# A real transform of 576 points along D, split 9 x 64 on VectorE and TensorE instead of 6 x 96 on TensorE and VectorE

## The chip, the core and the metric

The kernel runs on one core of one Trainium2 chip. The metric is the device time of one execution in microseconds (us). An execution also leaves a profile: start and duration of every instruction on TensorE (PE for its products, PEld for the loads of its stationary operand), VectorE (DVE), ScalarE (ACT), GpSimd (POOL) and of every DMA issued from the queues of SP, ACT and POOL.

## The reference, cut to what matters

The program computes the output and all gradients of a gated mix of two branches over a 2048 x 576 activation `x`: a spectral branch (a real 2-D Fourier transform over both axes, a product with complex weights, and the transform back) and a gated feed-forward branch with a hidden width of 4608.

```python
def _A_ref(x, w_r, w_i):
    X = rfft2(x.astype(float32), axes=(-2, -1))
    X = X * (w_r + 1j * w_i)
    return irfft2(X, s=(S, D), axes=(-2, -1)).astype(bfloat16)

def _B_ref(x, w_gate, w_up, w_down):
    return (gelu(x @ w_gate) * (x @ w_up)) @ w_down

g = sigmoid((x * gate_w).sum(-1, keepdims=True))
out = g * _A_ref(x, ...) + (1 - g) * _B_ref(x, ...)
```

The backward pass needs the forward transform twice: of `x`, and of the incoming gradient scaled by the gate `g`. In both cases 16 row tiles of 128 rows are transformed, 32 in all, and the change is in that transform's part along D (576 points, 289 kept frequencies, real and imaginary).

## The kernel before

The program has two phases. The first takes 18 groups `g` of 256 hidden columns, four steps `m` each, 72 steps `pr` in all; a step handles 512 rows. Each step issues on TensorE, in a fixed order: the products for `z` (L466, L471), the products for the hidden activations `xy` (L475, L482), and then a list of jobs that build weight gradients of the group before in `wps` (L594, L612, L626). The second phase (from about 915 us) turns the hidden gradients back into activations (L1228).

The spectral branch rides along in the first phase as small units, called one by one from a list (`fft_next`). A forward row tile has two units. `u1` (L651 to L662) multiplies the row tile with a cosine and sine table over the rows: six products (L656), one for each residue class of the column number modulo 6, into a PSUM tile `pf`, which ScalarE copies to `Z` (L659 for `x`, L661 for the gradient). `u2` (L664 to L698) multiplies `Z` with the table over the columns, six products again (L670), ScalarE copies the sums to `ve` in fp32 (L676), and VectorE combines the six parts in 17 instructions (L678 to L697) into `Vt`, from where a DMA on SP's queue stores it (L698). The six classes are picked out of the natural rows beforehand by a ScalarE copy that reads every sixth element (`sort`, L727 for `x`, L729 for the gradient, where the gate is multiplied in).

What orders the work: all instructions of an engine run in program order, and the program order is written out by hand. Per step there are three units in this stage: one in the middle of the second half of `xy` (`between`, L1084), the others spread over the list of jobs by their weights (L1112 to L1116). How many units a step gets is said by `want` from the list `FIRST` (L950: none in steps 0 to 6, one by step 7, three by step 8) and a line from there. The sorting of a unit's rows is issued a step ahead by `sort_ahead` (L971), behind the copies of `z` (L494) or behind the last unit of the step.

One detail carries the rest: `z` and all `pf` tiles share one PSUM buffer (pool `pz`, one buffer of two banks; L458 and L645). TensorE cannot begin a `z` or a unit until the last reader of the one before has finished. The `wps` and `xy` tiles have two buffers each.

The tables are built at the start: `iotas` (L61), `build_F` (L120, VectorE work at the start, two ScalarE sines in step 6).

Of the kernel before, what the change touches and what calls it, by code (L numbers as in the profile page):

```python
# [9 lines left out]
ACT = mybir.ActivationFunctionType  # L10
ALU = mybir.AluOpType
BF16 = mybir.dt.bfloat16
F32 = mybir.dt.float32
I32 = mybir.dt.int32
MAGIC = 12582912.0
EPS_SCALE = 1.0 - 3e-7
# [3 lines left out]
S, D, DF = 2048, 576, 289  # L20
P, T = 128, 16
# [16 lines left out]
LO, HI = slice(0, 64), slice(64, 128)  # L38
LQ = 49
SIN60 = math.sqrt(0.75)  # L40


def eo(c):
# [18 lines left out]
def iotas(nc, res, unit):  # L62
    tb = Tables()
    G, V = nc.gpsimd, nc.vector
    kw = dict(allow_small_or_imprecise_dtypes=True)
    tb.halfpi = res.tile([P, 1], F32, name="halfpi")
    V.memset(tb.halfpi[:], math.pi / 2)
    tb.pi = res.tile([P, 1], F32, name="pi")
    V.memset(tb.pi[:], math.pi * EPS_SCALE)
    tb.warm = res.tile([P, 1], F32, name="warm")  # L70
    nc.scalar.activation(tb.warm[:], tb.halfpi[:], ACT.Sigmoid)
    tb.lrow = unit([LQ], F32, name="lrow")
    G.iota(tb.lrow[:], pattern=[[1, LQ]], base=0, channel_multiplier=0, **kw)
    tb.dcol = res.tile([P, 6], F32, name="dcol")
    for k, (r, step, n) in enumerate(((1, 1, 2), (0, 0, 1), (5, -1, 3))):
        k0 = (0, 2, 3)[k]
        G.iota(tb.dcol[:, k0:k0 + n], pattern=[[step, n]], base=r, channel_multiplier=6, **kw)
    tb.late = []
    tb.Rt = []
    return tb  # L80
# [39 lines left out]
def build_F(nc, tb, unit):  # L120

    V = nc.vector
    step = 2.0 * math.pi / D
    X = unit([6, LQ], F32, name="XF")
    y = unit([6, LQ], F32, name="yF")
    V.tensor_tensor(X[:], tb.dcol[:].unsqueeze(2).to_broadcast([P, 6, LQ]), tb.lrow[:].unsqueeze(1).to_broadcast([P, 6, LQ]), op=ALU.mult)
    V.tensor_scalar(y[:], X[:], 1.0 / D, MAGIC, op0=ALU.mult, op1=ALU.add)
    V.tensor_scalar(y[:], y[:], -MAGIC, -float(D), op0=ALU.add, op1=ALU.mult)
    V.tensor_tensor(X[:], X[:], y[:], op=ALU.add)
    V.scalar_tensor_tensor(y[:], X[:], -1.0, X[:], op0=ALU.mult, op1=ALU.max)  # L130
    tb.F = unit([6, 2, LQ], name="Ft")

    def sines():
        nc.scalar.activation(tb.F[:, :, 0], y[:], ACT.Sin, bias=tb.halfpi[:], scale=-step)
        nc.scalar.activation(tb.F[:, :, 1], X[:], ACT.Sin, scale=-step * EPS_SCALE)
    tb.late.append(sines)


# [153 lines left out]
def kernel(  # L292
# [4 lines left out]
    nc = tc.nc  # L297
    LD = nc.sync
    ST = nc.gpsimd
    V = nc.vector  # L300
    ctx.enter_context(tc.manual_schedule())
    kw = dict(reuse_waits="tile")
    dram = ctx.enter_context(tc.tile_pool(name="dram", bufs=1, space=DRAM))
    res = ctx.enter_context(tc.tile_pool(name="res", bufs=1))
    unit = Unit(ctx.enter_context(tc.tile_pool(name="unit", bufs=NUNIT, side="right")), "unit")
# [25 lines left out]
    xn = wstack.enter_context(tc.tile_pool(name="pxn", bufs=1)).tile([P, T, D], BF16, name="xn")  # L331
# [51 lines left out]
    tb = iotas(nc, res, unit)  # L383
# [17 lines left out]
    g32 = res.tile([P, T], F32, name="g32")  # L401
# [244 lines left out]

    def fwd_units(src, dst, scale):
        zs = {}
        CLS = (1, 2, 0, 5, 4, 3)

        def u1(t):  # L651
            def f():
                zps = pftile()
                row = src.pop(t)
                for k, r in enumerate(CLS):
                    nc.tensor.matmul(zps[0:96, k // 3, k % 3 * P:(k % 3 + 1) * P], lhsT=row[:, r], rhs=tb.Rt[t], start=True, stop=True)  # L656
                zs[t] = unit([2, 3 * P], name="Z")
                if scale is None:
                    nc.scalar.copy(zs[t][0:96], zps[0:96, :, 0:3 * P])  # L659
                else:  # L660
                    nc.scalar.activation(zs[t][0:96], zps[0:96, :, 0:3 * P], ACT.Copy, scale=scale)  # L661
            return f  # L662

        def u2(t):  # L664
            def f():
                Z = zs.pop(t)
                vps = pftile()
                w = 2 * LQ
                for k in range(6):
                    nc.tensor.matmul(vps[:, k // 3, k % 3 * w:(k % 3 + 1) * w], lhsT=Z[0:96, k // 3, k % 3 * P:(k % 3 + 1) * P],  # L670
                                     rhs=tb.F[0:96, k].rearrange("p c l -> p (c l)"), start=True, stop=True)
                Vt = half([2, DF], name="Vt")
                ve = unit([2, 3, 2, LQ], F32, name="ve")
                sd = unit([2, 3, 2, LQ], F32, name="sd")
                M = unit([6, 2, LQ], F32, name="vm")
                nc.scalar.copy(ve[:].rearrange("p b k c l -> p b (k c l)"), vps[:, :, 0:3 * w])  # L676
                lo, hi = ve[:, 0], ve[:, 1]
                V.tensor_tensor(sd[:, 0], lo, hi, op=ALU.add)  # L678
                V.tensor_tensor(sd[:, 1, :, 0], hi[:, :, 0], lo[:, :, 0], op=ALU.subtract)
                V.tensor_tensor(sd[:, 1, :, 1], lo[:, :, 1], hi[:, :, 1], op=ALU.subtract)  # L680
                e, o = sd[:, 0, 2], sd[:, 1, 2]
                for k, op in enumerate((ALU.add, ALU.subtract)):
                    V.tensor_tensor(M[:, k], sd[:, 0, 0], sd[:, 0, 1], op=op)
                    V.tensor_tensor(M[:, 4 + k, 1::-1], sd[:, 1, 0], sd[:, 1, 1], op=op)
                p_, m_ = M[:, 0], M[:, 1]
                for c, op in enumerate((ALU.subtract, ALU.add)):
                    V.scalar_tensor_tensor(M[:, 2, c], m_[:, c], 0.5, o[:, c], op0=ALU.mult, op1=op)
                V.scalar_tensor_tensor(M[:, 3], p_, -0.5, e, op0=ALU.mult, op1=ALU.add)
                up = Vt[:, :, 96:DF - 1].rearrange("p c (j l) -> p j c l", j=2)[:, :, :, 0:LQ]
                dn = Vt[:, :, 1:193].rearrange("p c (j l) -> p j c l", j=2)[:, :, :, 94:47:-1]  # L690
                V.tensor_tensor(Vt[:, :, 0:LQ], e, p_, op=ALU.add)
                V.scalar_tensor_tensor(Vt[:, 0, DF - 1:DF - LQ:-1], o[:, 0, 0:LQ - 1], -1.0, m_[:, 0, 0:LQ - 1], op0=ALU.mult, op1=ALU.subtract)
                V.tensor_tensor(Vt[:, 1, DF - 1:DF - LQ:-1], m_[:, 1, 0:LQ - 1], o[:, 1, 0:LQ - 1], op=ALU.subtract)
                for c in range(2):
                    V.scalar_tensor_tensor(up[:, :, c], M[:, 4:6, c], SIN60, M[:, 2:4, c], op0=ALU.mult, op1=ALU.add)
                for c, s_, op in ((0, -SIN60, ALU.add), (1, SIN60, ALU.subtract)):
                    V.scalar_tensor_tensor(dn[:, :, c], M[:, 4:6, c, 1:LQ - 1], s_, M[:, 2:4, c, 1:LQ - 1], op0=ALU.mult, op1=op)  # L697
                LD.dma_start(dst[:, t], Vt[:])  # L698
            return f
        first = [u1(t) for t in range(T)]  # L700
        for t, u in enumerate(first):
            u.sort = (src, t)
        return first, [u2(t) for t in range(T)]

    xq, gq, graw = {}, {}, {}
# [2 lines left out]
        f.noslot = True  # L708
        return f

    def classes(dst, k):
        q = unit([2, 6, 96], name="xq")
        for j in range(2):
            dst[2 * k + j] = q[:, j]
        return q

    def load_g(k):
        def f():
# [2 lines left out]
        return noslot(f)  # L721

    def sort(dst, t):
        if t % 2 == 0:
            classes(dst, t // 2)
        if dst is xq:
            nc.scalar.copy(xq[t], xn[:, t, :].rearrange("p (q r) -> p r q", r=6))  # L727
        else:
            nc.scalar.activation(gq[t], graw[t // 2][:, t % 2].rearrange("p (q r) -> p r q", r=6), ACT.Copy, scale=g32[:, t:t + 1])  # L729

    def turned():
        tp_ = pftile(BF16)
# [159 lines left out]
    for c in range(6):  # L892
        w = gwr[0:1, eo(c)] if c < 4 else gwr[0:1, 512:D]
        r = slice(0, P) if c < 4 else (LO, HI)[c - 4]
# [52 lines left out]
    mid_at = 4 * T + 8  # L947
    NPR = NT // 2
    LASTP = NG * NPR - 7
    FIRST = (0, 0, 0, 0, 0, 0, 0, 1, 3)  # L950
    done = [0]

    def want(pr):
# [12 lines left out]
        return int(min(n, n_slots) + 1e-9)  # L966

    slots = [u for u in fft if not getattr(u, "noslot", False)]
    sorted_to = [0]

    def sort_ahead(pr):  # L971
        to = want(pr + 1) if pr + 1 < NG * NPR else n_slots
        due = [u.sort for u in slots[sorted_to[0]:to] if hasattr(u, "sort")]
        sorted_to[0] = max(to, sorted_to[0])
        n = int(pr != 7)
        for q in due[:n]:
            sort(*q)
        return due[n:]

    wgT_all = []  # L980

# [18 lines left out]
    for g in range(NG):  # L1000
# [3 lines left out]
        for m in range(NPR):  # L1004
            pr = g * NPR + m
            n = want(pr) - done[0]
# [64 lines left out]
            else:  # L1071
# [8 lines left out]
                k0 = int(n > 0 and pr > 7 and ready())  # L1080
# [23 lines left out]
                at, k, free = 0.0, k0, 0.0  # L1104
# [4 lines left out]
                if pr == 8:  # L1109
                    last = 1.2  # L1110
                    due = [d - last for d in due]
# [88 lines left out]
    with tc.tile_pool(name="p2f", bufs=3, **kw) as p2f, \  # L1200
# [36 lines left out]
        vp, ft, zt = {}, {}, {}  # L1237
# [239 lines left out]
```

## Time and profile before

| | us |
|---|---|
| median of the runs | 1361.12 (1360.99 to 1361.24, 3 runs) |
| the profiled execution: its own time | 1361.22 |
| its span, first to last instruction | 1359.4 |
| PE busy | 1343.9 (99%) |
| DVE busy | 879.5 (65%) |
| ACT busy | 771.0 (57%) |
| stretch with the forward units, 85 to 367 us: PE / DVE / ACT busy of 282.0 | 279.4 / 247.0 / 231.5 |

A row of the groups reads: line, engine, operation, output<-inputs, shape, count, then the busy time of the group, the mean of one, and the idle time of the engine just before. A row of the timeline reads: start, length, engine, line, what, and in square brackets the idle time of the engine before it and who ended it. Products are pipelined, so the records of two of them overlap; the time from start to start is what TensorE spends on one.

### The profile page before, as it was taken

How to read it: one execution, taken by the hardware profiler on the slowest of the kernel's cores; microseconds unless marked ns; L12 is line 12 of the kernel's file. 1: busy time of each engine (PE TensorE's matmuls, PEld its weight loads, DVE VectorE, ACT ScalarE, POOL GpSimd, SP SyncE). 2: the span in 40 equal slices, each digit the busy share in tenths (PEclk: the TensorE clock that was granted, in tenths of full speed). 3: DMA queues.
4: the chain of work that ended last, by engine and by line, in shares of the span. 5: the costliest groups of instructions: out<-in, count | busy, mean ns of one | idle time of the engine just before them, and what ended most of it. 6: DMA issues, size and time to landing. Idle time of an engine off the chain costs nothing.

```text
span 1359.4 us, 26947 instructions
## 1 busy us (share of the span) xinstructions
PE 1343.9 (99%) x10279; PEld 901.0 (66%) x10360; DVE 879.5 (65%) x2351; ACT 771.0 (57%) x1380; POOL 244.1 (18%) x488
## 2 busy tenths in 40 slices
PE   9999999999999999999999999999999999999999
PEld 6556656656655656655655655558888888888887
DVE  6988888888857876876776855526543455354420
ACT  5797888888767776776777666622332232232210
POOL 3011111110313633434433311100000000000000
PEclk9999999999999999999999999999999999999999
DMA  9624435534554644644754657499999787888773
GB/s 222 174 71 133 138 98 150 157 99 133 138 144 115 175 121 117 171 119 121 174 140 115 163 123 181 120 238 237 201 204 216 160 175 160 168 164 173 155 155 74
DMA packets 493606, 207.05 MB, mean 152 GB/s; under 512 B 313346, under 2 KB 485444, under 8 KB 493476
## 3 DMA queue, kind: packets, MB, share of 16 engines
q1 hardware_dynamic: 467330, 170.47, 55.1%
q0 software_dynamic: 15040, 24.38, 6.2%
q10 hardware_dynamic: 11106, 10.48, 3.1%
q8 instruction: 81, 1.33, 0.4%
q14 instruction: 49, 0.40, 0.1%
HBM read 41.18 MB, written 89.11 MB: 96 GB/s over the span
## 4 chain that ended last, share of the span: by engine, by line
PE 98%; DVE 1%; issue 1%; ACT 0%; ACTq 0%; DVEq 0%
PE acc L1228 31%; PE wps L612 18%; PE xy L482 18%; PE wps L594 10%; PE z L466 9%; PE wps L626 2%; PE xy L475 2%; PE z L471 2%; PE pf L656 1%; PE acc L1280 1%; PE pf L670 1%; PE acc L1290 1%; PE pf L856 1%; PE pf L778 1%; PE pf L419 0%
## 5 line engine op out<-in xcount | busy, mean ns | idle before, releaser
L1228 PEld LDWEIGHTS <-pin 128*128 128x128 bf16 x3456 | 334.7, 98 | 82.7
L482 PE MATMUL xy<-wgu,xT 128*128 128x512 bf16 x1082 | 257.8, 380 | 8.6 <-issue 7.4
L612 PE MATMUL wps<-dH,xn 128*128 128x512 bf16 x1141 | 263.8, 379 | 0.6
L612 PEld LDWEIGHTS <-xn 128*128 128x128 bf16 x1152 | 111.2, 98 | 125.5 <-issue 0.6
L482 PEld LDWEIGHTS <-xT 128*128 128x128 bf16 x1152 | 105.5, 98 | 133.2 <-issue 25.2
L594 PE MATMUL wps<-dB,A 128*128 128x288 bf16 x1152 | 149.9, 286 | 0.0
L619 POOL DMA_DIRECT2D out_dram<-dw x134 | 73.1, 549 | 423.5 <-ACT dw L563 411.8
L1228 PE MATMUL acc<-wgT,pin 128*128 128x288 bf16 x1152 | 146.6, 286 | 0.0
L1228 PE MATMUL acc<-wd_all,pin 128*128 128x288 bf16 x1152 | 146.4, 286 | 0.0
L1228 PE MATMUL acc<-wuT,pin 128*128 128x288 bf16 x1152 | 146.1, 286 | 0.0
L1292 ACT ACTIVATE yo<-acc 128x288 bf16<-128x288 f32 x64 | 67.4, 1245 | 132.2 <-PE acc L1290 113.3
L466 PE MATMUL z<-wdT,dOT 128*128 128x256 bf16 x1152 | 138.0, 273 | 0.9 <-ACT dOT L438 0.8
L594 PEld LDWEIGHTS <-A 128*128 128x128 bf16 x1152 | 111.7, 98 | 33.0
L494 ACT ACTIVATE da<-z,omg 128x256 bf16<-128x256 f32 x288 | 111.9, 471 | 28.3 <-PE z L471 28.1
L466 PEld LDWEIGHTS <-dOT 128*128 128x128 bf16 x1152 | 112.3, 98 | 22.6 <-issue 0.5
L1408 DVE TENSOR_TENSOR b16t<-acc,f32t 128x288 bf16<-128x288 f32 x32 | 14.7, 458 | 168.4 <-PE acc L1228 168.3
L503 ACT CAST xb<-xy 128x512 bf16<-128x512 f32 x144 | 85.6, 594 | 38.7 <-PE xy L482 38.0
L1282 ACT CAST Z<-acc 98x384 bf16<-98x384 f32 x64 | 27.5, 481 | 113.1 <-PE acc L1280 113.1
L504 ACT CAST hu<-xy 128x512 bf16<-128x512 f32 x144 | 87.9, 610 | 0.0
L540 DVE TENSOR_TENSOR xb<-xb,sg 128x1024 bf16<-128x1024 bf16 x48 | 33.1, 690 | 80.8 <-ACT sg L532 80.8
L501 ACT ACTIVATE q<-xy 128x512 bf16<-128x512 f32 x144 | 80.4, 606 | 3.3 <-PE xy L482 3.0
L563 ACT CAST dw<-wps 128x512 bf16<-128x512 f32 x72 | 42.2, 588 | 60.1 <-PE wps L612 42.8
(513 smaller groups left out, 1807.6 us busy)
## 6 DMA issues: line engine op xcount, KB each, us to landing
scr<-dH SPq DMA_DIRECT2D x144, 256.0 KB, 3.4
scr<-A SPq DMA_DIRECT2D x72, 256.0 KB, 2.4
out_dram<-dw POOLq DMA_DIRECT2D x134, 64.0 KB, 1.9
wd_all<-in_B_w_down_dram SPq DMA_DIRECT2D x3, 1728.0 KB, 12.6
out_dram<-dwd POOLq DMA_DIRECT2D x34, 144.0 KB, 2.9
scr_p<-Vt SPq DMA_DIRECT2D x32, 144.5 KB, 2.9
Vp<-scr_p ACTq DMA_DIRECT2D x32, 144.5 KB, 4.3
wgu<-in_B_w_gate_dram SPq DMA_DIRECT2D x18, 256.0 KB, 4.3
```

Source lines behind the costliest of these rows:

```text
L466: nc.tensor.matmul(zo(t), lhsT=dOT[:, ci, t, :], rhs=wdT[:, ci, :], start=(t % 4 < 2 and ci == 0), stop=False)
L482: nc.tensor.matmul(xy[k][:, t % 2, :], lhsT=xT[:, ci, t, :], rhs=wgu[:, ci, :], start=False, stop=(ci == 3))
L494: nc.scalar.activation(da[:, t, :], z[:, t % 2, t // 2, :], ACT.Copy, scale=omg32[:, 4 * m + t:4 * m + t + 1])
L501: nc.scalar.activation(q[:, h, :], xy[:, :, 0:FG], ACT.Square)
L503: nc.scalar.copy(xb[:, h, :], xy[:, :, 0:FG])
L504: nc.scalar.copy(hu[:, h, :], xy[:, :, FG:2 * FG])
L563: wcopy[0](out, in_)
L594: nc.tensor.matmul(wps[:, :288], lhsT=tl(0, t)[:, fch * P:(fch + 1) * P], rhs=dB[:, t, h * 288:(h + 1) * 288], start=(t == 0), stop=(t == ...
L612: nc.tensor.matmul(wps[:].rearrange("p a b -> p (a b)"), lhsT=xn[:, t, c * P:(c + 1) * P], rhs=kt[t // 4][1][:, t % 4].rearrange("p k f -> ...
L619: wst[0].dma_start(ov[:, c, fsl], dw[:, k, :])
L1228: nc.tensor.matmul(acc[:, :288], lhsT=src[:, r, :], rhs=w_of(r)[:, h * 288:(h + 1) * 288], start=(first and r == 0), stop=(last and r == F ...
L1292: nc.scalar.activation(yv[:, 3 * b:3 * b + 3], ps[:, 0:288].rearrange("p (r q) -> p r q", r=3), ACT.Copy, scale=(SD2, 1.0)[w])
```

## The change

The split of D becomes 9 x 64. The nine-point part moves to the front: `sort` no longer copies; VectorE computes the nine-point transform of two natural row tiles at a time from `xn` or `graw`, in `nine_a` (sums and cosines, 14 instructions) for the even tile of the pair and `nine_b` (differences and sines, 10 instructions) for the odd one, in fp32, into a tile `xq` of 64 + 4 x 128 columns per row. For the gradient, ScalarE first scales both natural rows of the pair in place. `u1` then has five products with 128 stationary columns, and two ScalarE copies into `Z` (512 and 128 columns). `u2` has four products of 128 columns with the rotations in the table and one of 66. There is no combining on VectorE any more: two ScalarE copies write `Vt` straight from PSUM, in frequency order, so that both step through `Vt` in steps of nine elements. The tables are built to match, `FIRST` becomes nine zeros, and `sort_ahead` counts sorts instead of slots (pairs are completed, and at most one sort is done beyond the need).

```diff
-                for k, r in enumerate(CLS):
-                    nc.tensor.matmul(zps[0:96, k // 3, k % 3 * P:(k % 3 + 1) * P], lhsT=row[:, r], rhs=tb.Rt[t], start=True, stop=True)
-                zs[t] = unit([2, 3 * P], name="Z")
-                if scale is None:
-                    nc.scalar.copy(zs[t][0:96], zps[0:96, :, 0:3 * P])
...
+                for k in (1, 2, 3, 4, 0):
+                    c0 = 128 * k - (64 if k else 0)
+                    nc.tensor.matmul(zps[:, int(k == 0), max(k - 1, 0) * P:max(k, 1) * P], lhsT=row[:, c0:c0 + P], rhs=tb.Rt[t], start=True, stop=True)
+                Z = zs[t] = unit([5 * P], name="Z")
+                for b, c in enumerate((slice(0, 4 * P), slice(4 * P, 5 * P))):
+                    if scale is None:
+                        nc.scalar.copy(Z[:, c], zps[:, b, 0:c.stop - c.start])
...
-                for k in range(6):
-                    nc.tensor.matmul(vps[:, k // 3, k % 3 * w:(k % 3 + 1) * w], lhsT=Z[0:96, k // 3, k % 3 * P:(k % 3 + 1) * P],
-                                     rhs=tb.F[0:96, k].rearrange("p c l -> p (c l)"), start=True, stop=True)
+                o = vps[:, 0].rearrange("p (c o q) -> p c o q", c=2, o=8)
+                for k in range(1, 5):
+                    nc.tensor.matmul(o[:, :, k - 1:9 - k:9 - 2 * k, :], lhsT=Z[:, (k - 1) * P:k * P],
+                                     rhs=tb.F[:, (k - 1) * P:k * P].rearrange("p (c h q) -> p c h q", c=2, h=2), start=True, stop=True)
+                nc.tensor.matmul(vps[:, 1, 0:66], lhsT=Z[:, 4 * P:5 * P], rhs=tb.F[:, 512:578], start=True, stop=True)
                 Vt = half([2, DF], name="Vt")
-                nc.scalar.copy(ve[:].rearrange("p b k c l -> p b (k c l)"), vps[:, :, 0:3 * w])
...
+                nc.scalar.copy(Vt[:, :, 0:DF - 1].rearrange("p c (q o) -> p c o q", o=9)[:, :, 1:9, :], o)
+                nc.scalar.copy(Vt[:, :, 0:DF:9], vps[:, 1, 0:66].rearrange("p (c q) -> p c q", c=2))
                 LD.dma_start(dst[:, t], Vt[:])
...
+    def nine_a(q, x, d):
+        Y = unit([3, 2, 64], F32, name="nY")
+        W = unit([3, 2, 64], F32, name="nW")
+        sm = unit([4, 2, 64], F32, name="nS")
+        s3, e, m, sg = (sm[:, k] for k in range(4))
+        V.tensor_tensor(Y[:], x[:, 1:8:3], x[:, 8:1:-3], op=ALU.add)
+        V.tensor_tensor(s3, x[:, 3], x[:, 6], op=ALU.add)
+        V.tensor_tensor(e, x[:, 0], s3, op=ALU.add)
+        V.scalar_tensor_tensor(m, s3, -0.5, x[:, 0], op0=ALU.mult, op1=ALU.add)
+        V.tensor_tensor(W[:, 0:2], Y[:, 0:2], Y[:, 1:3], op=ALU.subtract)
+        V.tensor_tensor(W[:, 2], Y[:, 2], Y[:, 0], op=ALU.subtract)
+        V.tensor_tensor(sg, Y[:, 0], Y[:, 1], op=ALU.add)
+        V.tensor_tensor(sg, sg, Y[:, 2], op=ALU.add)
+        V.tensor_tensor(q, e, sg, op=ALU.add)
+        V.scalar_tensor_tensor(d[:, 2, :, 0], sg, -0.5, e, op0=ALU.mult, op1=ALU.add)
+        V.scalar_tensor_tensor(Y[:], W[:], C1, m.unsqueeze(1).to_broadcast([P, 3, 2, 64]), op0=ALU.mult, op1=ALU.add)
+        for k, j in ((0, 0), (1, 1), (3, 2)):
+            V.scalar_tensor_tensor(d[:, k, :, 0], W[:, (j + 1) % 3], -C2, Y[:, j], op0=ALU.mult, op1=ALU.add)
...
     def sort(dst, t):
-        if t % 2 == 0:
-            classes(dst, t // 2)
-        if dst is xq:
-            nc.scalar.copy(xq[t], xn[:, t, :].rearrange("p (q r) -> p r q", r=6))
-        else:
-            nc.scalar.activation(gq[t], graw[t // 2][:, t % 2].rearrange("p (q r) -> p r q", r=6), ACT.Copy, scale=g32[:, t:t + 1])
+        k, h = t // 2, t % 2
+        if h == 0:
+            q = pairs[k] = unit([2, D], name="xq")
+            for j in range(2):
+                dst[2 * k + j] = q[:, j]
+                if dst is gq:
+                    nc.scalar.activation(graw[k][:, j], graw[k][:, j], ACT.Copy, scale=g32[:, 2 * k + j:2 * k + j + 1])
+        q = pairs[k]
+        x = xn[:, 2 * k:2 * k + 2, :] if dst is xq else graw[k][:]
+        (nine_a, nine_b)[h](q[:, :, 0:64], x.rearrange("p t (j r) -> p j t r", j=9),
+                            q[:, :, 64:D].rearrange("p t (k v r) -> p k t v r", k=4, v=2))
...
-    FIRST = (0, 0, 0, 0, 0, 0, 0, 1, 3)
+    FIRST = (0,) * 9
...
-        due = [u.sort for u in slots[sorted_to[0]:to] if hasattr(u, "sort")]
+        need = sum(1 for u in slots[:to] if hasattr(u, "sort"))
+        need += need % 2
+        to = max(need, min(sorted_to[0] + 1, need + 1, len(sorts)) if pr > 6 else 0)
+        due = sorts[sorted_to[0]:to]
         sorted_to[0] = max(to, sorted_to[0])
-        n = int(pr != 7)
-        for q in due[:n]:
+        for q in due[:1]:
             sort(*q)
-        return due[n:]
+        return due[1:]
```

In `iotas` and `build_F`, four iotas on POOL become eight with four small memsets on VectorE, the column table has 578 columns instead of 6 x 2 x 49, and ScalarE makes one sine over 578 columns and two scaled copies instead of two sines over 294.

More of the change, by code (lines that the diff above doesn't have):

```diff
@@ L40 @@
 SIN60 = math.sqrt(0.75)
+C1, C2 = (math.cos(2.0 * math.pi * k / 9) for k in (1, 2))
+S1, S4 = (math.sin(2.0 * math.pi * k / 9) / SIN60 for k in (1, 4))
+TURN = 4.0 * MAGIC
 def eo(c):
@@ L71, in iotas @@
     nc.scalar.activation(tb.warm[:], tb.halfpi[:], ACT.Sigmoid)
[L72 to L77, printed above, removed]
+    ft = tb.ft = unit([P], F32, name="ft")
+    G.iota(ft[:, 0:33], pattern=[[9, 33]], base=0, channel_multiplier=0, **kw)
+    o16 = ft[:, 40:56].rearrange("p (k c h) -> p k c h", k=4, c=2)
+    t16 = ft[:, 56:72].rearrange("p (k c h) -> p k c h", k=4, c=2)
+    for h in range(2):
+        G.iota(o16[:, :, :, h], pattern=[[1 - 2 * h, 4], [0, 2]], base=(1, 8)[h], channel_multiplier=0, **kw)
+    G.iota(t16[LO], pattern=[[0, 4], [1, 2], [0, 2]], base=3, channel_multiplier=0, **kw)
+    G.iota(t16[HI, 0:4:3], pattern=[[0, 2], [1, 2], [-2, 2]], base=2, channel_multiplier=0, **kw)
+    G.iota(t16[HI, 1:3], pattern=[[0, 2], [1, 2], [2, 2]], base=0, channel_multiplier=0, **kw)
+    for k, r in enumerate((LO, HI)):
+        G.iota(ft[r, 72:73], pattern=[[0, 1]], base=0, channel_multiplier=1, **kw)
+    tb.fsc = res.tile([P, 2], F32, name="fsc")
+    for r, v in ((LO, (1.0, 1.0)), (HI, (SIN60, 0.0))):
+        for c in range(2):
+            V.memset(tb.fsc[r, c:c + 1], v[c])
     tb.late = []
@@ L122, in build_F @@
     V = nc.vector
[L123 to L131, printed above, removed]
+    ft = tb.ft
+    row, o16, t16, r_ = ft[:, 0:33], ft[:, 40:56], ft[:, 56:72], ft[:, 72:73]
+    X = unit([578], F32, name="XF")
+    y = unit([578], F32, name="yF")
+    V.tensor_scalar(r_, r_, 4.0 / D, None, op0=ALU.mult)
+    V.scalar_tensor_tensor(t16, o16, r_, t16, op0=ALU.mult, op1=ALU.add)
+    V.tensor_scalar(row, row, r_, None, op0=ALU.mult)
+    V.tensor_tensor(X[:, 0:512].rearrange("p (k q) -> p k q", q=32), t16.unsqueeze(2).to_broadcast([P, 16, 32]),
+                    row[:, 0:32].unsqueeze(1).to_broadcast([P, 16, 32]), op=ALU.add)
+    for c in range(2):
+        V.tensor_scalar(X[:, 512 + 33 * c:545 + 33 * c], row, 3.0 + c, None, op0=ALU.add)
+    V.tensor_scalar(y[:], X[:], TURN, None, op0=ALU.add)
+    V.scalar_tensor_tensor(X[:], y[:], -TURN, X[:], op0=ALU.add, op1=ALU.subtract)
+    tb.F = unit([578], name="Ft")
     def sines():
-        nc.scalar.activation(tb.F[:, :, 0], y[:], ACT.Sin, bias=tb.halfpi[:], scale=-step)
-        nc.scalar.activation(tb.F[:, :, 1], X[:], ACT.Sin, scale=-step * EPS_SCALE)
+        nc.scalar.activation(X[:], X[:], ACT.Sin, scale=0.5 * math.pi * EPS_SCALE)
+        for c, r in enumerate((slice(0, 512), slice(512, 578))):
+            nc.scalar.activation(tb.F[:, r], X[:, r], ACT.Copy, scale=tb.fsc[:, c:c + 1])
     tb.late.append(sines)
@@ L648, in fwd_units @@
         zs = {}
-        CLS = (1, 2, 0, 5, 4, 3)
         def u1(t):
@@ L654, in f @@
                 row = src.pop(t)
-                for k, r in enumerate(CLS):
-                    nc.tensor.matmul(zps[0:96, k // 3, k % 3 * P:(k % 3 + 1) * P], lhsT=row[:, r], rhs=tb.Rt[t], start=True, stop=True)
-                zs[t] = unit([2, 3 * P], name="Z")
-                if scale is None:
-                    nc.scalar.copy(zs[t][0:96], zps[0:96, :, 0:3 * P])
-                else:
-                    nc.scalar.activation(zs[t][0:96], zps[0:96, :, 0:3 * P], ACT.Copy, scale=scale)
+                for k in (1, 2, 3, 4, 0):
[5 more added lines that the diff above has]
+                        nc.scalar.copy(Z[:, c], zps[:, b, 0:c.stop - c.start])
+                    else:
+                        nc.scalar.activation(Z[:, c], zps[:, b, 0:c.stop - c.start], ACT.Copy, scale=scale)
             return f
@@ L667, in f @@
                 vps = pftile()
-                w = 2 * LQ
-                for k in range(6):
-                    nc.tensor.matmul(vps[:, k // 3, k % 3 * w:(k % 3 + 1) * w], lhsT=Z[0:96, k // 3, k % 3 * P:(k % 3 + 1) * P],
-                                     rhs=tb.F[0:96, k].rearrange("p c l -> p (c l)"), start=True, stop=True)
-                Vt = half([2, DF], name="Vt")
-                ve = unit([2, 3, 2, LQ], F32, name="ve")
-                sd = unit([2, 3, 2, LQ], F32, name="sd")
-                M = unit([6, 2, LQ], F32, name="vm")
@@ L676, in f @@
[L676 to L697, printed above, removed]
+                o = vps[:, 0].rearrange("p (c o q) -> p c o q", c=2, o=8)
@@ L709, in noslot, with nine_b @@
         return f
[L711 to L715, printed above, removed]
+    def nine_a(q, x, d):
[16 more added lines that the diff above has]
+            V.scalar_tensor_tensor(d[:, k, :, 0], W[:, (j + 1) % 3], -C2, Y[:, j], op0=ALU.mult, op1=ALU.add)
+    def nine_b(q, x, d):
+        Y = unit([3, 2, 64], F32, name="nY")
+        W = unit([3, 2, 64], F32, name="nW")
+        sm = unit([2, 2, 64], F32, name="nS")
+        V.tensor_tensor(Y[:], x[:, 1:8:3], x[:, 8:1:-3], op=ALU.subtract)
+        V.tensor_tensor(sm[:, 0], x[:, 3], x[:, 6], op=ALU.subtract)
+        V.tensor_tensor(W[:, 1:3], Y[:, 0:2], Y[:, 1:3], op=ALU.subtract)
+        V.tensor_tensor(W[:, 0], Y[:, 2], Y[:, 0], op=ALU.subtract)
+        V.tensor_tensor(sm[:, 1], Y[:, 0], Y[:, 1], op=ALU.add)
+        V.tensor_tensor(d[:, 2, :, 1], sm[:, 1], Y[:, 2], op=ALU.add)
+        V.scalar_tensor_tensor(Y[:], W[:], S1, sm[:, 0].unsqueeze(1).to_broadcast([P, 3, 2, 64]), op0=ALU.mult, op1=ALU.subtract)
+        for k, j in ((0, 0), (1, 1), (3, 2)):
+            V.scalar_tensor_tensor(d[:, k, :, 1], W[:, (j + 2) % 3], -S4, Y[:, j], op0=ALU.mult, op1=ALU.add)
+    pairs = {}
     def load_g(k):
@@ L723, in sort @@
     def sort(dst, t):
-        if t % 2 == 0:
-            classes(dst, t // 2)
-        if dst is xq:
-            nc.scalar.copy(xq[t], xn[:, t, :].rearrange("p (q r) -> p r q", r=6))
-        else:
-            nc.scalar.activation(gq[t], graw[t // 2][:, t % 2].rearrange("p (q r) -> p r q", r=6), ACT.Copy, scale=g32[:, t:t + 1])
+        k, h = t // 2, t % 2
[9 more added lines that the diff above has]
+                            q[:, :, 64:D].rearrange("p t (k v r) -> p k t v r", k=4, v=2))
     def turned():
@@ L968 @@
     slots = [u for u in fft if not getattr(u, "noslot", False)]
+    sorts = [u.sort for u in slots if hasattr(u, "sort")]
     sorted_to = [0]
```

## The prediction

> **What bounds the kernel now.** I read the page from its ends: the chain of work that ended last, then what TensorE (PE) waited for, then the rows of the lines that change.
>
> ```profile
> PE 98%; DVE 1%; issue 1%; ACT 0%; ACTq 0%; DVEq 0%
> ```
>
> The list of PE's waits has hardly anything in it; the longest sums are these.
>
> ```profile
> PE xy L482 <- issue: 7.4, 47, 0.2
> PE pf L885 <- DVE pi L69: 1.1, 1, 1.1
> ```
>
> The reader is to see that the time is the sum of PE's products, and that nothing on the other engines is late. So a change can gain only what it takes from PE, and can lose whatever makes PE wait. All forward units lie between 84 and 362 us; in 85 to 367 us VectorE (DVE) is busy 247.0 and ScalarE (ACT) 231.5 of 282.0 us.
>
> **PE: what the units cost.** The busy sums (16.0 us for 192 products of u1, 83 ns each) count the pipeline's tail. The timeline shows the real price:
>
> ```profile
> 275.65 0.50 PE L656 MATMUL pf<-Rt,xq 128*96 128x128 bf16 x6
> ...
> 275.98 0.60 PE L612 MATMUL wps<-dH,xn 128*128 128x512 bf16 x2
> ```
>
> From the start of u1 to the start of the next group it takes 0.33 us: six times 0.056. The same between u2 at 224.23 and the next group at 224.50: 0.27 us, six times 0.045 for 98 columns. Transposes with 128 stationary and 128 moving columns (L419 at 10.37: 16 in 1.06 us, one taking 0.219) also start every (1.06 - 0.22)/15 = 0.056 us. Hence five products of 128 columns are 0.28, and four of 128 with one of 66 (on the slope between 0.045 and 0.056, some 0.032) are 0.256 us. A tile falls from 0.606 to 0.536; 32 tiles give **-2.3 us**. That is all PE can gain here. Whether the output of u2, scattered over PSUM in runs of 32, slows a product, no row shows; I take 0, with at most a doubling of 4 x 0.056 x 32 = +7 us as the other end.
>
> **DVE: as much work as before.** DVE instructions overlap: those of u2 start 279.08 (L678) and end 282.17 (L697), 3.1 us a tile, though their durations sum to 4.4. From start to start, 294 elements take 0.38, 147 take 0.22 and 98 take 0.17 us, thus 0.07 us plus 1.05 ns an element. nine_a has two of 384 elements (0.47 each), one of 256 (0.34) and eleven of 128 (0.20): 3.5 us; nine_b two, one and seven: 2.7 us. A pair costs 6.2 us, a tile 3.1. So no change in the sum; bounds are 2.3 (if an element costs 0.67 ns, as in the two-byte L510, 0.69 us for 1024) and 4.1 (no overlap). It runs a step ahead of its u1, which covers it.
>
> **ACT: where the change costs.** The sort goes: 1.01 us a tile for x, 1.10 for the gradient (0.88 and 0.98 from start to start). Scaling the gradient's rows adds 0.70 (L996: 128x576 in 0.81, less 0.11 of overlap). Z in two copies is 0.48 + 0.27 against 0.80: equal. But the copies into Vt step by nine two-byte elements, 18 bytes. The only row with such writes is L1292, which steps by six, 12 bytes; L1350 writes as many elements without a step:
>
> ```profile
> L1292 ACT ACTIVATE yo<-acc 128x288 bf16<-128x288 f32 x64 | 67.4, 1245 | 132.2 <-PE acc L1290 113.3 <-DMA do_t<-in_grad_out_dram 19.0
> L676 ACT COPY ve<-pf 128x588 f32<-128x588 f32 x32 | 21.2, 664 | 0.7 <-PE pf L670 0.3
> L1350 ACT CAST bo<-acc 128x288 bf16<-128x288 f32 x32 | 13.4, 434 | 24.2 <-PE acc L1228 23.4 <-issue 0.8
> ```
>
> Two of them back to back, from the timeline:
>
> ```profile
> 1013.15 2.10 ACT L1292 ACTIVATE yo<-acc 128x288 bf16<-128x288 f32 x2 [3.79 <-PE acc L1290]
> ```
>
> 576 stepped elements in two instructions take 2.10 us. The new pair writes 512 + 66 = 578: **2.1 us where ve took 0.66, so 1.45 us more** until PSUM is free. From below: written at the plain rate (512 in 0.59, started on by 66 after 0.48) it is 0.7, or +0.05. From above: if the price grows with the step, 0.18 + 1.92 x 18/12 = 3.1, or +2.4. I take 1.45, by the row that matches in engine, type and count.
>
> The Trainium skill, "SBUF — State Buffer", section "Door 1: The DMA port swizzle", speaks against the change: SBUF has 16-byte lines, and an access that crosses to a new line pays unless each line gets two hits. By that rule a step of 18 bytes never hits a line twice, a step of 12 does so for one element in four, so L1292 even flatters the new copy: priced by line (216 lines in 0.96 us, an estimate from that page's line size) 578 lines are 2.6 + 0.2 = 2.8 us, 2.1 more than ve; the covers counted below would leave about 30 us of stall instead of 12, and the sum would end some 18 us higher than mine.
>
> **Who waits.** z and all pf tiles share one PSUM buffer, so the next z or unit on PE waits for that copy. The cover is small:
>
> ```profile
> 277.71 0.43 PE L670 MATMUL pf<-Ft,Z 96*128 96x98 bf16 x6
> ...
> 278.39 0.66 ACT L676 COPY ve<-pf 128x588 f32<-128x588 f32 x1
> ...
> 279.71 1.91 PE L466 MATMUL z<-wdT,dOT 128*128 128x256 bf16 x16
> ```
>
> The copy ends at 279.05 and z starts at 279.71: cover 0.66 us. Walking the timeline over all 32 u2 units, nine have 0.55 to 0.66, seven 0.85 to 0.90, nine 1.08 to 1.33, seven 1.74 or more. With 1.45 us more, PE stalls by the rest: 7.5 + 4.0 + 2.5 + 0 = 14.0 us. Three units fewer by step 8 move u1 and u2 into each other's places, until a step with four units (3.08 per step now) moves them back at about step 21. In u1's places sixteen covers are 0.50 to 0.73, five 0.95 to 0.97, eleven 1.52 or more, each 0.2 longer for a u2 (its copy 0.14, its products 0.06 shorter): 10.3 us. Half of each: **12 us**.
>
> Then what is queued behind the copy on ACT. At 297.10 u2 runs inside xy; behind its copy stand L501, L503, L504 without a gap, then Z of the next u1 (300.50), which the u2 at 302.02 reads. These all slip by about 1.4 us; PE, itself 0.2 late, waits for Z 0.5 us where it waited for nothing. About ten steps of 21 are of this kind: 5 us, less some, since the 1.0 us sort ahead of L503 in these steps is gone: **+4 us**. ACT's sum grows by 32 x 1.45 - 16 x 0.88 - 16 x 0.98 + 16 x 0.70 = 28 us, to 259 of some 296: dense, not full. With no stall at all ACT hides everything, and this costs 0.
>
> **The small edits.** At the start four more iotas (some 0.12 us each, L73 and L77) and four memsets make build_F end near 4.6 instead of 4.0 us; the next DVE work (5.13) waits for PE anyway. The tail loads of POOL's queue (L386) leave 0.5 us later than 1.69 to 3.9, and L475 needs them at 13.30. Tables in step 6 cost ACT 0.6 us more, and the unit that came after in step 7 is gone. Vt's store on SP's queue (L698) goes out earlier, not later, for it no longer stands behind 3.1 us of DVE. All 0; each would cost its own length if the cover went.
>
> **Sum.** 1361.2 (the profiled execution: span 1359.4 and 1.8 around it; 0.1 above the median of the runs) - 2.3 + 12 + 4 = **1375 us**.
>
> **The rivals.**
> 1. *The stepped copy at the plain rate.* Then no cover is used up and only PE's 2.3 us remain: 1359, not slower. It decides at +0.55 us, the smallest cover. For it: L1292 is a row of the second phase, in another stretch of DMA load, with another step. Against: L1350 in the same stretch takes 0.40 us. A price between (+0.7 to +1.1) costs 0.4 to 5 us of stall: 1360 to 1364.
> 2. *The step of 18 is dearer than that of 12.* At +2.05 us the covers leave 31 and 25 us, mean 28, and at +2.4 us 39, and more slips on: 1361 - 2 + 28 + 5 = 1392, up to 1403.
> 3. *DVE becomes the bound.* nine_a stands ahead of L509 in steps where no u2 stood there; at 287.32 L509 waited 0.22 us for q only. If each of 21 steps ran 0.4 us late into its sigmoid, and so into z's copies, it is 8 us on top of rival 1: 1367. Against: the sum of DVE's work is the same.
>
> **How the numbers follow.** Forecast (+1.2 to +1.8 us; 1367 to 1382): 0.57. Dearer: 0.17. Rival 1 with the prices between: 0.20. Rival 3: 0.06. A measurement here can tell 0.2%, 2.7 us, from no change. PE's gain of 2.3 stays within that, so of rival 1's 0.20 I give 0.05 to faster (PE gains somewhat more than I see), 0.14 to same and 0.01 to slower; with the other three, slower is 0.81. The range takes in rival 1 and most of the dearer case: 1359 to 1394.
>
> **What would show it.** The copies into Vt at 1.8 to 2.0 us (512 elements) and about 0.4 (66); ACT as releaser of PE's waits before z L466, u1 and u2, some 16 us in sum between 95 and 375 us, and none later; five starts 0.056 us apart in u1; DVE 3.1 us a tile ahead of u1. Copies under 1.2 us together, or PE waiting for DVE before u1, would make it wrong.

## The result, and the profile after

The changed kernel takes 1407.3 us (median of five runs, 1405.2 to 1409.7) against 1361.1: a ratio of 1.034, with a 95% interval of 1.0329 to 1.0353. The forecast was 1375 us, range 1359 to 1394: the right side, and far too little. The profiled execution took 1409.56 us, 1407.8 from first to last instruction, 48.4 more than before.

The chain of work that ended last, in shares by engine, now has ScalarE in it:

```profile
PE 81%; ACT 8%; issue 2%; DVE 1%; SPq 0%; DMA 0%; ACTq 0%; DVEq 0%
```

The list of TensorE's waits (who waits, for whom: us in total, how often, the longest) has gained these lines:

```profile
PE pf L674 <- ACT Vt L694: 16.7, 17, 2.8
PE z L484 <- ACT Vt L694: 9.3, 10, 1.1
...
PE pf L674 <- ACT da L512: 3.3, 1, 3.3
PE pf L689 <- ACT Z L680: 2.9, 5, 1.4
PE pf L689 <- ACT Z L678: 2.6, 4, 0.9
PE z L484 <- DMA wdT<-in_B_w_down_dram: 1.7, 1, 1.7
PE pf L689 <- ACT Vt L694: 1.5, 2, 0.9
PE wps L612 <- DVE A L557: 1.2, 1, 1.2
PE pf L674 <- DVE s L528: 1.1, 1, 1.1
```

L674 and L689 are now the products of u1 and u2, L693 and L694 the two copies into Vt, L484 the products of z; da is ScalarE's copy of z, and s and A are VectorE's tiles of the hidden activations. Three kinds are to be told apart: 27.5 us for Vt (the stepped copies themselves), 5.5 for Z (what is queued behind them), and 5.6 for da, A and s (late work on VectorE, see below). The 1.7 us for wdT, a tile of weights, stand by themselves at 42.4 us, ahead of all forward units. A product's record lasts about 0.2 us (0.219 for 128 columns that start every 0.056), and so hides some 0.16 us of each wait: measured from start to start, the three kinds are about 32, 7 and 6 us.

The two copies, as groups:

```profile
L693 ACT CAST Vt<-pf 128x512 bf16<-128x512 f32 x32 | 78.4, 2450 | 3.2 <-PE pf L691 2.2
...
L694 ACT CAST Vt<-pf 128x66 bf16<-128x66 f32 x32 | 25.7, 803 | 0.0
```

2.45 us for 512 elements, and the pair is through after 2.72 us (0.66 before). How this meets the cover, from the timeline:

```profile
204.52 2.43 ACT L693 CAST Vt<-pf 128x512 bf16<-128x512 f32 x1 [0.50 <-PE pf L691]
...
206.46 0.78 ACT L694 CAST Vt<-pf 128x66 bf16<-128x66 f32 x1
...
207.29 1.91 PE L484 MATMUL z<-wdT,dOT 128*128 128x256 bf16 x16 [1.07 <-ACT Vt L694]
```

The copy ends at 207.24, and z starts 0.05 us later, after an idle time of 1.07 us.

TensorE's own work did shrink. A u1 in the timeline:

```profile
212.48 0.44 PE L674 MATMUL pf<-Rt,xq 128*128 128x128 bf16 x5
...
212.76 1.03 PE L500 MATMUL xy<-wgu,xT 128*128 128x512 bf16 x4
```

From its start to the next group 0.28 us, where it was 0.33. Over all units the medians are 0.277 against 0.335 for u1 and 0.252 against 0.274 for u2: 0.080 us a tile, 2.6 us in all.

Then the stretches of half clock, which the kernel before doesn't have (stretch, its length, busy time of each engine, and behind POOL the granted clock, DMA share and GB/s):

```profile
105.00:108.00 3.00, 0.00 (x0) 0.00 (x0) 2.67 (x5) 2.97 (x6) 0.00 (x0) 0.87 0.63 160
108.00:111.00 3.00, 2.80 (x12) 1.49 (x12) 2.96 (x6) 2.63 (x7) 0.00 (x0) 0.50 0.26 53
111.00:114.40 3.40, 3.40 (x20) 2.17 (x19) 3.26 (x14) 1.25 (x4) 0.00 (x0) 0.55 0.00 0
114.50:118.00 3.50, 3.50 (x35) 2.83 (x33) 3.36 (x10) 2.32 (x5) 0.54 (x1) 1.00 0.15 49
```

TensorE stood idle from 104.9 to 108.2, and its clock was halved for 6.8 us, from 107.2 to 114.1; another 3.4 us at half clock follow the wait of 2.8 us that ends at 264.2. TensorE worked through 5.9 and 3.4 us of them, so the work lost is 0.5 x 9.3 = 4.6 us. With the wait for wdT (1.8 from start to start) the sum is -2.6 + 32 + 7 + 6 + 4.6 + 1.8 = +48.8 us; the profile shows 48.4. The wait for wdT is not shown to come from the change: in the profiles of the experiments on the changed kernel it is 1.1, 0.3, 0.2 or missing.

### The profile page after: what moved, and what is told of

It reads as the page before. It is cut to its first block, busy times and chain, and to the rows that moved or that the text cites. A ratio compares the mean times of both kernels' runs of the same rounds, so it can differ in the third digit from the quotient of the medians.

```text
span 1407.8 us, 26803 instructions
## 1 busy us (share of the span) xinstructions
PE 1352.4 (96%) x10215; PEld 899.2 (64%) x10296; DVE 891.6 (63%) x2197; ACT 818.0 (58%) x1430; POOL 245.4 (17%) x492
## 3 DMA queue, kind: packets, MB, share of 16 engines
q8 instruction: 80, 1.31, 0.4%
## 4 chain that ended last, share of the span: by engine, by line
PE 81%; ACT 8%; issue 2%; DVE 1%; SPq 0%; DMA 0%; ACTq 0%; DVEq 0%
PE acc L1262 30%; PE xy L500 14%; PE wps L630 14%; PE wps L612 7%; PE z L484 7%; ACT Vt L693 3%; PE wps L644 2%; PE xy L493 2%; PE z L489 1%; ACT Vt L694 1%; PE acc L1314 1%; PE acc L1324 1%; ACT xb L521 1%; PE pf L674 1%; PE pf L887 1%
## 5 line engine op out<-in xcount | busy, mean ns | idle before, releaser
L484 PE MATMUL z<-wdT,dOT 128*128 128x256 bf16 x1152 | 138.0, 273 | 11.9 <-ACT Vt L694 9.3
L484 PEld LDWEIGHTS <-dOT 128*128 128x128 bf16 x1152 | 112.1, 98 | 35.8 <-issue 12.6
L1316 ACT CAST Z<-acc 98x384 bf16<-98x384 f32 x64 | 27.5, 481 | 111.9 <-PE acc L1314 111.9
L519 ACT ACTIVATE q<-xy 128x512 bf16<-128x512 f32 x144 | 84.1, 630 | 4.0 <-PE xy L500 3.7
L693 ACT CAST Vt<-pf 128x512 bf16<-128x512 f32 x32 | 78.4, 2450 | 3.2 <-PE pf L691 2.2
```

Of the source, the lines that this page charges most:

```text
L484: nc.tensor.matmul(zo(t), lhsT=dOT[:, ci, t, :], rhs=wdT[:, ci, :], start=(t % 4 < 2 and ci == 0), stop=False)
L519: nc.scalar.activation(q[:, h, :], xy[:, :, 0:FG], ACT.Square)
L693: nc.scalar.copy(Vt[:, :, 0:DF - 1].rearrange("p c (q o) -> p c o q", o=9)[:, :, 1:9, :], o)
```

## The experiments

Each was run beside the kernel before (1361.0 to 1361.1 us there). Theory A: the stepped copies hold the one PSUM buffer. Its rival, theory B: the nine points stand on VectorE in front of `H_ew1`, the first work on the hidden activations (L527 to L531), the sigmoid on ScalarE comes late, and all behind it. Experiments 1, 3 and 5 leave the frequencies in another order, so what they compute from them is not the reference's.

**1. The copies written in plain order.**

```diff
-                nc.scalar.copy(Vt[:, :, 0:DF - 1].rearrange("p c (q o) -> p c o q", o=9)[:, :, 1:9, :], o)
-                nc.scalar.copy(Vt[:, :, 0:DF:9], vps[:, 1, 0:66].rearrange("p (c q) -> p c q", c=2))
+                nc.scalar.copy(Vt[:, :, 0:256], vps[:, 0].rearrange("p (c x) -> p c x", c=2))
+                nc.scalar.copy(Vt[:, :, 256:DF], vps[:, 1, 0:66].rearrange("p (c q) -> p c q", c=2))
```

> The changed kernel, but both copies into Vt write one element after the other (the frequencies then stand in another order, so all that is computed from them changes). Theory A, the stepped writes hold the shared PSUM buffer 2.06 us longer per u2 (2.72 against 0.66): the copies take 0.6 and 0.3 us, PE's waits for Vt (27.5 us) go, most of those for Z (5.5) too; what is left are the waits that came from late DVE work (da 3.3, A 1.2, s 1.1) and the slower clock after the first of them (some 3.4): 1362 to 1370. Theory B, nine_a and nine_b stand in front of the hidden activations' first DVE work (L527, L528), ScalarE stands at the sigmoid and everything behind it is late: the stepping hardly matters, the time stays above 1390.

1366.7 us, ratio 1.0044 (1.0028 to 1.0061). The pair of copies takes 0.71 us, no wait for Vt is left, and one wait for Z (0.9). So 41 of the 46 us hang on the stepping: the waits, what queues behind them, and the second stretch of half clock. The waits for da (3.3) and A (1.2) are still there, and 3.4 us of half clock with the wait for da (6.8 in the changed kernel, with the same wait). The wait for s (1.1) is gone, though nothing on VectorE was moved: it needed the stepped copies too.

**2. The sort issued behind H_ew1.**

```diff
-                unsorted = sort_ahead(pr)
...
                 state += [*H_ew1(g, tiles, da), da]
+                unsorted = sort_ahead(pr)
```

> The changed kernel with the step's first sort issued behind H_ew1 instead of before it; nothing else. Theory A: only the waits of late DVE work and what hangs on them go (da 3.3, A 1.2, s 1.1, 3.4 of slower clock): 1397 to 1400; PE still waits some 27 us for Vt. Theory B: below 1375.

1415.1 us, ratio 1.0398 (1.0383 to 1.0414): a miss, and to the wrong side. The steps show why. Step 15 begins 7.0 us earlier than in the changed kernel (185.6 against 192.6), as theory B would have it for x; step 27 begins 3.6 us later (376.9 against 373.3). In the gradient's half the sort has ScalarE work as well, and that was moved too. From the timeline:

```profile
254.58 1.46 ACT L756 ACTIVATE graw<-graw,g 128x576 bf16<-128x576 bf16 x2
255.92 0.59 ACT L581 CAST dw<-wps 128x512 bf16<-128x512 f32 x1
256.39 2.44 ACT L693 CAST Vt<-pf 128x512 bf16<-128x512 f32 x1
258.30 0.81 ACT L694 CAST Vt<-pf 128x66 bf16<-128x66 f32 x1
```

The scaling of two rows now stands in front of a stepped copy whose products had ended by 253.3; the u1 behind it waited 4.1 us, to 259.16, and the clock was halved from 258.1 on. Three more stretches follow, 6.8 + 3 x 3.4 us in all. TensorE worked through 15.9 us of them, some 8 us of lost work where the changed kernel loses 1.7 in that half. So the clock costs more there than the waits, which are 4 us longer from start to start (31.4 against 27.5 from 225 us on).

**3. Both edits at once.**

> Both edits at once (frequencies in another order, as in the plain writes). Theory A and B together: no wait is left but those of the kernel before, and PE's own gain shows: 1358.5 to 1360. If something else in the change costs (the shifted units, the tables at the start, products that write scattered runs of PSUM): 1362 or more, and the profile shows PE products further apart than 0.056 us, or a wait of another kind.

1369.1 us, ratio 1.0056 (1.0041 to 1.0071), 9 us above the expectation. No product is further apart than expected; the waits are of another kind. 1.8 us are for Vt behind the moved scaling, 0.9 for A, 0.9 for Z, 0.6 for da, and about 2.9 us stand in the second phase (from 915 us), where nothing was changed: PE waits once 2.0 us for a copy of bo, and twice 0.4 to 0.5.

**4. The same places written, with the loops swapped.**

```diff
-                nc.scalar.copy(Vt[:, :, 0:DF - 1].rearrange("p c (q o) -> p c o q", o=9)[:, :, 1:9, :], o)
+                nc.scalar.copy(Vt[:, :, 0:DF - 1].rearrange("p c (q o) -> p c q o", o=9)[:, :, :, 1:9],
+                               vps[:, 0].rearrange("p (c o q) -> p c q o", c=2, o=8))
```

> The changed kernel, the 512-element copy with its two inner loops swapped: the same elements go to the same places, but eight neighbours in a row are written (16 bytes), and it is the reads from PSUM that step, by 32 fp32 elements. If the price is one for each new line of SBUF that a write meets (as in the skill's SBUF page), the copy meets about 128 lines instead of 512: some 0.6 to 0.9 us, with the 66-element copy 1.0 to 1.3 until PSUM is free, and the time is 1366 to 1375. If any stepping costs, on the reading side too, the copy stays above 2 us and the time above 1400.

1368.7 us, ratio 1.0054 (1.0039 to 1.0069). The large copy, as a group:

```profile
L693 ACT CAST Vt<-pf 128x512 bf16<-128x512 f32 x32 | 19.7, 616 | 3.1 <-PE pf L691 2.3
```

0.62 us in the mean, 0.60 in the median: as fast as the plain one (0.60), though each read from PSUM now steps by 128 bytes. The small copy still writes in steps, and the pair takes 0.94 us (0.71 in plain order). It is the writes that cost, not the stepping as such, and one line of code gives back 39 us with the same result in the same places.

**5. A ladder of steps.** The large copy written with `"p c (x k) -> p c k x"`, k = 1, 2, 4, 8, 16, 32 in turn.

> The changed kernel, the large copy written with another step in each row tile (1, 2, 4, 8, 16 and 32 elements of two bytes in turn, read from PSUM in plain order), the small copy plain; the frequencies stand in another order. A price for each new 16-byte line, as the skill's SBUF page has it with two hits a line for nothing: 0.6 us for steps of 1, 2 and 4, and 2.3 to 2.5 us for 8, 16 and 32. A price that grows with the step: a rise from each to the next, and 32 far above 2.4 us. A price for any step other than one: 2.4 us from step 2 on.

The first copies of each step, in that order, from the timeline (1379.6 us for the whole, one run):

```profile
114.19 0.60 ACT L694 CAST Vt<-pf 128x512 bf16<-128x512 f32 x1
...
126.30 0.74 ACT L694 CAST Vt<-pf 128x512 bf16<-128x512 f32 x1
...
135.49 1.31 ACT L694 CAST Vt<-pf 128x512 bf16<-128x512 f32 x1
...
140.39 2.45 ACT L694 CAST Vt<-pf 128x512 bf16<-128x512 f32 x1 [0.50 <-PE pf L691]
...
151.47 2.37 ACT L694 CAST Vt<-pf 128x512 bf16<-128x512 f32 x1
...
161.82 2.44 ACT L694 CAST Vt<-pf 128x512 bf16<-128x512 f32 x1
```

Steps of 2, 4, 8, 16, 32 and 64 bytes. The price rises up to 16 bytes and is flat from there, so it is paid per 16 bytes touched: 128, 256 and 512 such lines cost 0.74, 1.31 and 2.45 us, 4.4 ns for each further line. None of the three expected prices fits whole: the first is right from 8 elements on, but had steps of 2 and 4 elements for nothing. The Trainium skill, "SBUF — State Buffer", section "Door 1: The DMA port swizzle", names 16-byte lines, and the runs agree; it also says that two hits a line are enough for full bandwidth, and here two hits (8 bytes) still cost 2.2 times the plain copy, and four hits (4 bytes) 1.2 times.

**6. The shift of the units alone.** The kernel before with `FIRST = (0,) * 9` (and without the exception for step 7 in `sort_ahead`).

> The kernel before with the list FIRST of nine zeros (three units fewer by step 8, the rest a little denser) and none of the rest of the change. If the shift of the units costs nothing, as the forecast has it: 1360.5 to 1362. If it is part of the rest that is left in the runs so far (5 to 8 us): 1364 or more.

1361.5 us, ratio 1.0006 (0.9997 to 1.0015): the shift costs nothing that can be told. One of its ten runs took 1365.5, and it is the one with the profile: PE waits 2.7 us in the second phase, for a DMA into pin and for a copy of bo, and has half the clock for 3.4 us behind them.

**7. The stepped copies kept, the sort split.** `sort_ahead` only scales (and allocates), the first nine-point half follows H_ew1.

```diff
+        for q in due:
+            prepare(*q)
+        return due
...
                 state += [*H_ew1(g, tiles, da), da]
+                if unsorted:
+                    sort(*unsorted.pop(0))
```

> The changed kernel with its stepped copies, the gradient's scaling where it was, and the first nine-point half of the step behind H_ew1. The run with the whole sort moved lost in the gradient's half what it won in that of x. If that was the scaling (two copies of 0.8 us) standing in front of the stepped copy on ScalarE, this run keeps the win: 1397 to 1401. If it was the later nine points: 1405 or more again.

1403.1 us, ratio 1.0309 (1.0294 to 1.0325), between the two expectations: 4.2 us below the changed kernel, and 12 below experiment 2, from which it differs by where the scaling stands. The wait for da fell from 3.3 to 0.2, s is gone. So it was the place of the scaling that cost experiment 2 its win. 2 us of the win expected are not seen; 1.9 us of waits stand in the second phase. The waits for Vt are what they were:

```profile
PE pf L674 <- ACT Vt L694: 17.4, 18, 2.8
PE z L484 <- ACT Vt L694: 9.5, 10, 1.1
```

**8. Swapped loops and split sort: the best version found.**

> The changed kernel with the loops of the large copy swapped, the gradient's scaling left where it was on ScalarE, and the first nine-point half of the step behind H_ew1 instead of before it. If the stepped writes (A) and the nine points ahead of the gelu chain (B) are all that the change costs, only some 1 us of waits for A at step 8 stays against PE's gain of 2.3: 1359 to 1361. If not, 1364 or more.

1364.3 us (seven runs, 1362.2 to 1366.1), ratio 1.0027 (1.0016 to 1.0038): 3 us above the expectation, on the side that says that A and B are not all, and still above the kernel before. Its waits beyond those of the kernel before:

```profile
PE acc L1332 <- ACT bo L1392: 2.0, 1, 2.0
...
PE wps L612 <- DVE A L557: 0.9, 1, 0.9
...
PE pf L689 <- ACT da L512: 0.4, 1, 0.4
PE pf L689 <- ACT Z L680: 0.4, 1, 0.4
```

With the small ones 2.2 us in the first phase eat PE's gain of 2.6 (more from start to start), and 2.0 stand in the second. There ScalarE, which also issues loads, went from issuing do_t at 989.1 to issuing Vp at 993.3 without work, and the copies behind were late; in the kernel before the same two issues are 0.6 us apart. Why the issue stalls in some executions is open. The kernel before shows no such wait in its profile, and all its runs lie within 1.3 us. From the first product into acc to the end, the second phase lasts 446.4 us in five of the ten profiles (the kernel before, the changed one, experiments 1, 2 and 5) and 448.3 to 451.0 in the other five (3, 4, 6, 7 and 8). Experiment 6 has no nine points at all, so they are not needed for it.

No version that was run beats the kernel before. Two more versions have an expectation and no result: experiment 8 with the units begun one more step later, which would take the first nine points out of the way of the A at step 8 (expected 1363 to 1364, or 1359 to 1360), and copies of just the 2.1 us that the forecast had assumed (expected 1372 to 1377 if its covers were counted rightly). So it stays open what either would give.

## Why the forecast was wrong, point by point

**PE's gain.** -2.3 forecast, -2.6 measured. The price from start to start, not from the busy sums, was the right one, and output scattered in runs of 32 costs nothing (0.056 us a product).

**The step that failed: "2.1 us where ve took 0.66, so 1.45 us more ... by the row that matches in engine, type and count".** It was 2.72, so 2.06 more. The yo row was the right row, but its count was the wrong thing to carry over. At a step of 12 bytes, 288 elements touch 216 lines of 16 bytes, at 4.4 ns 0.95 us, and 0.18 us of start make its 1.14; at 18 bytes each of the 578 elements touches a line of its own: 2.5 + 0.2 = 2.7. The sentence on the skill's page in the forecast had this price (2.8), and it was set aside for the row. Both were needed: the row gives the ns, the rule what they are counted by. The mechanism was the right one; the size of this term was wrong, and it carries 23 of the 35 us between the forecast and the profiled execution: 32 + 7 us of stall and queue where 12 + 4 were added up. The rest is what the sum put at nothing: 6 us of late work on VectorE, 4.6 of half clock and the 1.8 for wdT.

**The covers.** With the size put right, the walk over the 32 covers holds to some 4 us: it gave 28 us of stall at +2.05, and 32 were measured from start to start (27.5 in the list of waits). What queues behind the copies, 4 to 5 us forecast, is 5.5 for Z in the list, 7 from start to start.

**ACT's sum.** 28 us more were forecast; it is 818.0 - 771.0 = 47. The 32 x 0.62 = 20 us by which the pairs of copies are longer than assumed account for the difference.

**DVE.** 3.1 us a tile were forecast. nine_a takes 4.06 us (213.30 to 217.36) and nine_b 3.08 (227.08 to 230.16), 3.6 a tile: small instructions that read what the one just before them wrote start 0.32 to 0.40 us after it, where 0.20 was counted. "It runs a step ahead of its u1, which covers it" was the second thing that failed: u1 was covered, but the work on the hidden activations, which the nine points stand in front of, was not. Its order mattered more than its sum, as rival 3 had it, but rival 3 was priced as another case, when it came on top. That its 8 us are near the 6 measured is chance: it counted 0.4 us in each of 21 steps, and the list shows three waits, of 3.3, 1.2 and 1.1 us. At step 9, from the timeline of the changed kernel:

```profile
102.69 0.69 DVE L739 SCALAR_TENSOR_TENSOR xq<-nW,nY 128x128 bf16<-128x128 f32 x3
103.30 0.42 DVE L527 TENSOR_SCALAR s<-q 128x1024 bf16<-128x1024 bf16 x1
...
103.83 0.69 DVE L528 TENSOR_TENSOR s<-xb,s 128x1024 bf16<-128x1024 bf16 x1
...
104.55 1.06 ACT L550 ACTIVATE sg<-s 128x1024 bf16<-128x1024 bf16 x1 [4.11 <-DVE s L528]
...
106.60 1.55 ACT L512 ACTIVATE da<-z,omg 128x256 bf16<-128x256 f32 x4
...
108.20 0.69 PE L674 MATMUL pf<-Rt,xq 128*128 128x128 bf16 x5 [3.28 <-ACT da L512]
```

nine_b ends, s is made, the sigmoid has stood 4.1 us at the head of ScalarE's queue, z is copied out behind it, and only then is the PSUM buffer free for u1. With the waits for A and s that is 6 us in all; experiment 7 leaves 0.2 for da and 0.9 for A.

**What was not in the forecast:** 4.6 us of half clock with the two longest waits.

**The rivals** were written as one or the other. Dearer copies alone gave 1392; the order on VectorE and the clock came on top, and the range ended below their sum.

**The small edits** at nothing: the shift of the units costs nothing that can be told (experiment 6). No experiment has the tables and the start alone; the first z begins no later (7.2 us against 7.8), and whether the wait for wdT at 42.4 belongs to them is open.

## What to carry to other kernels

A copy out of a PSUM buffer that has no second one is on TensorE's path, however idle ScalarE is in the mean: list for each use how long after the copy the next product wants the buffer, and hold the new copy's length against that list. Price a stepped two-byte write by the 16-byte lines it touches, and before moving the permutation elsewhere, swap the loops of the copy so that the reads from PSUM step and the writes run. Where work is put in front of an in-order engine's queue, follow what stands behind it through the next engine, and add up causes that can happen together instead of weighing them against each other.

## What the runs showed of the hardware

ScalarE writing two-byte elements to SBUF: 0.60, 0.74, 1.31, 2.45, 2.37 and 2.44 us for 512 elements at steps of 2, 4, 8, 16, 32 and 64 bytes. Reading fp32 from PSUM at a step of 128 bytes: 0.60 us, as in plain order. The 66 plain elements behind the 512 have a longer record after a step of 16 bytes (0.57 us, against 0.23 after none), but that is overlap and no further delay: their record starts 0.51 us before the large copy's ends (0.12 after a plain one), and the pair is through in 2.50 us.

TensorE at half clock for 6.8 us after an idle time of 3.3 us, and for 3.4 us after one of 2.8; the waits of 1.7 us and less in the same profile left the clock at 1.00 (280 to 367 us). The length of the one wait does not settle it: in experiment 2 half clock came with waits of 2.0 and 2.6 us (to 356.9 and 325.1) and not with others of 2.1 and 2.6 (to 242.5 and 389.7).
